# Retention attention and top-1 experts on one core: a token group's last tiles turned at the end of the next batch, and three PSUM tiles given other banks

## The chip, the core and the metric

The program runs on one core of one Trainium2 chip. The metric is the device time of that core in microseconds (us): 628.96 us, the median of three runs (627.0 to 629.3). The engines are named as the profile names them: PE (matrix products and transposes), DVE (vector engine), ACT (scalar engine), POOL (GpSimd), SP (the engine that issues most DMAs).

## The reference

```python
scores = scale * np.matmul(q, k.transpose(0, 1, 3, 2))      # 8 batches, 8 heads, 576 positions, head size 64
Dmat = np.where(rel >= 0, gamma[:, None, None] ** rel[None, :, :], 0.0)
ret = np.matmul(scores * Dmat[None], v)                     # no softmax: a decay by distance
x = ret.transpose(0, 2, 1, 3).reshape(B * S, H * D)         # 4608 tokens of 512
logits = xn @ en.T / tau                                    # 8 experts
expert_idx = np.argmax(logits, axis=1)
out[mask] = gate_w[mask, None] * (np.maximum(x[mask] @ w1[e], 0.0) @ w2[e])   # for each expert e
```

All is float32. The first part is linear attention with a decay; the second sends each token to one of eight experts, each of two weight matrices (512x1024 and 1024x512).

## The kernel before

**Two stages.** The first some 167 us are the attention, batch after batch; the rest are the eight experts, in which PE hardly pauses. The change lies in the attention.

**A batch.** Its 576 positions are four chunks of 128 and a tail of 64. Heads go in four pairs `p`. `emit_A(b, p)` (L584) makes the scores inside the chunks in two PSUM tiles `a` and DVE masks them (L599) into an SBUF tile `raw`. `emit_U(b)` (L607) makes k times v for each chunk, 32 products into two PSUM tiles `m`, which DVE sums up over the chunks into `Tst` (L627 once, L629 three times: the first of these frees the first of the two PSUM tiles, the third frees the second). `emit_QT` (L645) and `emit_O` (L663) add q times Tst and masked scores times v in a PSUM tile `o` per pair, and DVE scales it into `xT` and `xC` (`emit_X`, L677; lines L681, L683, L684). The tail has its own scores, `emit_At` (L686, masked by L695 into `pt`), and its own product, `emit_Ot` (L700): 16 products into two PSUM tiles, one for the even pairs and one for the odd, scaled by L722.

**The loop** (L809 to L860) runs over batches `b` and pairs `p`. At p = 0 the loads of batch b + 1 are issued and v of batch b + 1 is scaled on POOL (L567 four times, L571 once, `scale_v`). At p = 3 it already makes A and U of batch b + 1, since PE would else wait for their masks and sums. The load of v for batch b + 1 goes into the buffer that batch b - 1 used, so it waits for the tail product of b - 1.

**Token groups.** The tokens that batch b made are a group: 4 tiles of 128 tokens for an even batch, 5 for an odd one (`group_tiles`, L178). A group is worked off in the batch after its own, in tasks that `route_tasks` (L786) makes and the loop pops at the pairs in `SLOTS`: `route_logits` (L752), `route_tile` (L733: four transposes on PE into a PSUM tile `m`, a copy to SBUF on ACT, L744, a store to `xd` in DRAM by SP, L746, and a sum of squares on ACT, L748), `route_turn` (L766: the logits are transposed, DVE reduces them, L776), `route_head` (L182: six small DVE instructions, L194 to L202), `route_rank` and `route_onehot` (L243, L283) and `route_table` (L311). In each of batches 2 to 5 a quarter of the first expert's weights is split too: SP loads it, ACT rounds it (L168), DVE takes the rest (L169).

**Banks.** PSUM has eight banks: three tiles `a` (pool `psa`), two `o` (`pso`), three `m` (`psm`, shared by U, transposes, logits, tables and the tail). A tile takes a bank of its pool that another tile had before, and its first write waits until that tile has been read.

**Order.** Instructions are emitted in the loop's order, and a scheduler that goes by costs then interleaves them on each engine; each engine runs its row in that order, and waits where a semaphore has not come.

Of the kernel before, what the change touches and what calls it, by code (L numbers as in the profile page):

```python
# [9 lines left out]
F32 = mybir.dt.float32  # L10
# [8 lines left out]
P = 128  # L19
B, H, S, D = 8, 8, 576, 64  # L20
NP = H // 2
# [19 lines left out]
NW2 = 12  # L41
LAG = (3, 1)
POPS = (8, 3, 4, 0)
SLOTS = (0, 2)
NO = NT + 2


# [39 lines left out]
def retention_moe(ctx: ExitStack, tc: tile.TileContext, qk, kv, embT, tau, w1, w2, cst, out):  # L87
# [7 lines left out]
    psa = ctx.enter_context(tc.tile_pool(name="psa", bufs=3, space=PSUM))  # L95
# [20 lines left out]
    def behind():  # L116

        return ExitStack()
# [328 lines left out]
    with ExitStack() as att:  # L447
# [236 lines left out]
                nc.vector.tensor_tensor(out=x[:, p, : 512 - D], in0=po[:, D:], in1=gsb[:, p, D:512], op=ALU.mult)  # L684

        def emit_At(b):  # L686
            ps = psm.tile([P, 512], F32, name="m")
            u = ps[:, : NP * TL].rearrange("p (r n) -> p r n", r=NP)
            for p in range(NP):
                for h in range(2):  # L690
                    hs = slice(h * D, (h + 1) * D)
                    t = qkt[b, p]
                    mm(u[hs, p, :], t[hs, 1, 512:], t[hs, 0, 512:], start=True, stop=True)
            pt = a2.tile([P, NP, TL], F32, name="pt")
            nc.vector.tensor_tensor(  # L695
                out=pt, in0=u, in1=trit.unsqueeze(1).broadcast_to([P, NP, TL]), op=ALU.mult
            )
            Pt[b] = pt

        def emit_Ot(b):  # L700
            vt, T, pt = vtview(b), Tst[b % 2], Pt.pop(b)
            us = []
            for odd in range(2):
                ps = psm.tile([P, 512], F32, name="m")
                us.append(ps[:, : NP // 2 * TL].rearrange("p (r n) -> p r n", r=NP // 2))
            for r in range(NP // 2):
                for k in range(2):
                    for odd in range(2):
                        p = 2 * r + odd
                        for h in range(2):  # L710
                            hs = slice(h * D, (h + 1) * D)
                            mm(
                                us[odd][out_rows(p, h), r, :],
                                T[hs, NCH - 1, p, :] if k == 0 else vt[hs, p, :],
                                qkt[b, p][hs, 0, 512:] if k == 0 else pt[hs, p, :],
                                start=(r == 0 and k == 0),
                                stop=(r == NP // 2 - 1 and k == 1),
                            )
            x, xc = x_tiles(b)
            dst = xc[:, :, :TL] if b % 2 == 0 else x[:, :, 512 - D :]  # L720
            for odd in range(2):
                nc.vector.tensor_tensor(  # L722
                    out=dst[:, odd::2], in0=us[odd], in1=gsb[:, odd::2, 512:], op=ALU.mult
                )
# [27 lines left out]
        def route_logits(b):  # L752

            x = xT[b, "x"]
            lt = a1.tile([P, 5 * P], F32, name="lt")
            parts = [(x, 0, 512)] if b % 2 == 0 else [(x, P, 512), (xC[b // 2], 0, P)]
            for src, o, n in parts:
                ps = psm.tile([P, 512], F32, name="m")
                for p in range(NP):
                    mm(  # L760
                        ps[p * EW : (p + 1) * EW, :n], E32[:, p, :], src[:, p, :], start=True, stop=True
                    )
                nc.scalar.copy(lt[:, o : o + n], ps[:, :n])  # L763
            ltb[b] = lt
# [21 lines left out]
        def route_tasks(b):  # L786
            G = group_tiles(b)[1]
            tiles = [lambda g=g: route_tile(b, g) for g in range(G)]
            head = lambda: route_head(b)
            rank, table = (lambda: (route_rank(b), route_onehot(b))), (lambda: route_table(b))  # L790
            own = [lambda: route_logits(b)] + tiles[:2], tiles[2:] + [lambda: route_turn(b), head]

            first, second = owed or ([], [])
            owed[:] = [rank], [table]
            if b == B - 2:
                t = first + [lambda: (route_logits(b), route_turn(b))] + second + tiles[:2] + [head, rank]
                t += tiles[2:] + [table, lambda: slots_to_tokens(0, 3)]
                t += [lambda i=i: gather(0, i, group_tiles(B - 1)[0] * P) for i in range(3)]
                return t + [route_bump]
            return [own[0] + first, own[1] + second]  # L800

        tasks = []
        wq = wsplit_tasks(0)
# [5 lines left out]
        for b in range(B):  # L809
            for p in range(NP):  # L810
                if b + 1 < B:
                    load_qk(b + 1, p)
                    if p == 0:
                        load_v(b + 1)
                        load_k(b + 1)
                        scale_v(b + 1)
                if p + 1 < NP:
                    if b > 0 or p == 2:
                        with behind() if b > 0 else ExitStack():
                            emit_A(b, p + 1)  # L820
                else:
                    with behind():
                        if b + 1 < B:
                            emit_A(b + 1, 0)
                    with behind():
                        emit_At(b)
                    with behind():
                        if b + 1 < B:
                            emit_U(b + 1)
                if b == 0 and p == 0:  # L830
                    for r in range(NP):
                        turn_k(r)
                    emit_U(0)
                for _ in range(POPS[p] if b == B - 1 else 0):
                    if tasks:
                        tasks.pop(0)()
                if b == 0 and p < 2:
                    emit_O(b, p, True)
                    if p == 1:
                        emit_QT(b, 0, False)  # L840
                        emit_X(b, 0)
                        emit_X(b, 1)
                else:
                    if p % 2 == 0:
                        with behind():
                            emit_QT(b, p, True)
                    with behind() if b > 0 else ExitStack():
                        emit_O(b, p, False)
                    emit_X(b, p)
                if p == NP - 1:  # L850
                    with behind():
                        emit_Ot(b)
                if b < B - 1 and p in SLOTS and tasks:
                    with behind():
                        for task in tasks.pop(0):
                            task()
                if 1 < b < 6 and p == 1 and wq:
                    wq.pop(0)()
            if b < B - 1:
                tasks += route_tasks(b)  # L860
        b = B - 1
# [7 lines left out]
        first = [mm1_in(0, 0, 0)]  # L869
# [298 lines left out]
```

## Time and profile before

| | |
|---|---|
| median of the runs | 628.96 us (627.0 to 629.3) |
| the profiled execution | 627.92 us, span 626.1 us |
| PE busy | 609.4 us, 97% of the span |
| DVE, ACT, POOL busy | 54%, 35%, 29% |
| granted TensorE clock | 0.995 of 2.4 GHz in the mean |
| tail product ends, batches 1 to 6 | 47.96, 67.66, 87.69, 107.72, 127.96, 148.64 us |

In the timeline a row has the start, the time from the first start to the last end of the instructions merged in it, engine, line, operation, tiles (out<-in), their size and count; in brackets the engine's idle time just before and what ended it. A matmul in float32 leaves two records. Every product is recorded by the helper at L109 and every transpose by that at L113, so rows of PE are told apart by their tiles: `m<-ident,xT` is a token tile's transposes, `m<-ident,lt` those of the logits, `m<-rp,bt` the table, `a<-qkt` scores, `m<-qkt` (64x64) tail scores, `m<-vt,kt` U, `o<-raw,vt` the masked scores times v, `m<-qkt,Tst` and `m<-pt,vt` the tail product.

### The profile page before, as it was taken

The numbers are of one execution on the slowest core, as the hardware profiler recorded it, in microseconds if no ns is written. First come the engines' busy times: TensorE is split into PE (matmuls) and PEld (weight loads), VectorE is DVE, ScalarE is ACT, GpSimd is POOL, SyncE is SP. The second block draws the span as 40 slices with busy tenths as digits, with TensorE's granted clock in tenths as the row PEclk, the third lists the DMA queues.
The fourth block names the chain that finished last, engine by engine and source line by source line (L and its number), as shares of the span: only waits on it lengthen the run. The fifth ranks groups of instructions, "written<-read, shape, count | busy, mean of one in ns | idle before, by whom it ended". The sixth has DMA issues, their size and how long they took to land. (4 is left out here: it accounts for less than half of the span.)

```text
span 626.1 us, 12659 instructions
## 1 busy us (share of the span) xinstructions
PE 609.4 (97%) x5273; PEld 541.6 (87%) x5273; DVE 339.3 (54%) x687; ACT 216.7 (35%) x397; POOL 180.3 (29%) x165
## 2 busy tenths in 40 slices
PE   9999999989899999999999999999999999999995
PEld 8877778867698989889988998998899899889985
DVE  5676877768767776723670673368057426802200
ACT  1033333423444554423351433335143333512211
POOL 2522022220156636032313504241341324020011
PEclk9999999989999999999999999999999999999999
DMA  8899887972367895661483258147324824510001
GB/s 308 311 329 367 300 317 275 344 262 103 106 208 218 206 307 153 149 235 46 118 274 103 81 115 268 65 118 238 130 69 114 273 71 117 149 51 9 2 35 44
DMA packets 73275, 109.41 MB, mean 175 GB/s; under 512 B 44634, under 2 KB 45054, under 8 KB 71424
## 3 DMA queue, kind: packets, MB, share of 16 engines
q1 hardware_dynamic: 65536, 88.63, 44.1%
q0 software_dynamic: 7680, 19.95, 9.6%
q8 instruction: 42, 0.69, 0.4%
q14 instruction: 17, 0.14, 0.1%
HBM read 79.96 MB, written 19.94 MB: 160 GB/s over the span
## 5 line engine op out<-in xcount | busy, mean ns | idle before, releaser
L109 PE MATMUL a<-xs,wslot 128*128 128x384 f32 (+1 forms) x1536 | 227.8, 309 | 0.0
L109 PEld LDWEIGHTS a<-xs,wslot 128*128 128x128 f32 x1536 | 225.8, 189 | 0.7
L913 PE MATMUL o<-wslot,hs 128*128 128x512 f32 (+1 forms) x984 | 222.0, 386 | 0.0
L913 PEld LDWEIGHTS o<-wslot,hs 128*128 128x128 f32 x984 | 181.1, 188 | 38.3
L887 DVE SCALAR_TENSOR_TENSOR hs<-a,hs 128x384 fp32r<-128x384 f32 (+1 forms) x128 | 62.8, 490 | 170.6 <-ACT hs L886 167.8
L921 POOL DMA_INDIRECT out<-y,sid x40 | 43.4, 1086 | 225.1 <-ACT y L920 192.8
L886 ACT ACTIVATE hs<-a 128x384 fp32r<-128x384 f32 (+1 forms) x128 | 56.1, 439 | 127.3 <-PE a L109 117.3
L169 DVE TENSOR_TENSOR wslot<-raw,wslot 128x1024 fp32r<-128x1024 f32 x64 | 78.3, 1223 | 26.5 <-ACT wslot L168 25.4
L168 ACT CAST wslot<-raw 128x1024 fp32r<-128x1024 f32 x64 | 66.8, 1044 | 39.2 <-DMA raw<-w 39.2
L355 POOL DMA_INDIRECT raw<-xd,gid x40 | 41.6, 1041 | 88.8 <-DVE wslot L169 45.6
L920 ACT ACTIVATE y<-o,gt 128x512 f32<-128x512 f32 (+1 forms) x41 | 27.7, 677 | 110.5 <-PE o L913 94.7
L567 POOL TENSOR_TENSOR vt<-vt,cs 128x512 f32<-128x512 f32 x28 | 28.3, 1045 | 90.4 <-DMA vt<-kv 74.4
L366 POOL DMA_INDIRECT gt<-gd,gid x40 | 50.0, 1251 | 12.2 <-issue 12.2
L109 PE MATMUL a<-qkt 64*128 64x128 f32 x512 | 43.0, 291 | 2.5 <-DVE raw L599 2.5
L599 DVE TENSOR_TENSOR raw<-a,tri 128x512 f32<-128x512 f32 x64 | 41.4, 684 | 6.1 <-PE a L109 6.0
L109 PEld LDWEIGHTS a<-qkt 64*128 64x128 f32 x512 | 34.9, 189 | 7.5 <-DVE raw L599 3.9
L109 PE MATMUL o<-raw,vt 128*64 128x128 f32 x512 | 36.1, 280 | 0.0
L109 PEld LDWEIGHTS o<-raw,vt 128*64 128x64 f32 x512 | 28.2, 138 | 4.3 <-issue 3.2
L400 DVE COPY raw<-raw 128x1024 uint16<-128x1024 uint16 x37 | 28.2, 785 | 4.0 <-DMA raw<-raw 4.0
L744 ACT COPY y<-m 128x512 f32<-128x512 f32 x34 | 18.8, 586 | 32.5 <-PE m L113 32.4
L393 DVE COPY raw<-raw 128x1024 uint16<-128x1024 uint16 x37 | 26.0, 717 | 0.9 <-DMA raw<-xd,gid 0.9
L763 ACT COPY lt<-m 128x512 f32<-128x512 f32 (+1 forms) x12 | 5.4, 482 | 59.8 <-PE m L109 59.8
(127 smaller groups left out, 386.6 us busy)
## 6 DMA issues: line engine op xcount, KB each, us to landing
raw<-w SPq DMA_DIRECT2D x64, 512.0 KB, 4.8
qkt<-qk SPq DMA_DIRECT2D x32, 576.0 KB, 6.4
xd<-y SPq DMA_DIRECT2D x36, 256.0 KB, 3.5
vt<-kv SPq DMA_DIRECT2D x7, 1152.0 KB, 10.3
kt<-kv SPq DMA_DIRECT2D x7, 1024.0 KB, 5.0
vt<-kv SPq DMA_DIRECT2D x4, 256.0 KB
raw<-xd,gid POOLq DMA_INDIRECT x40
gt<-gd,gid POOLq DMA_INDIRECT x40
```

Source lines behind the costliest of these rows:

```text
L109: pe[:] = [nc.tensor.matmul(*args, **kw)]
L168: nc.scalar.copy(hi, raw)
L169: nc.vector.tensor_tensor(out=sl[:, 1, c * 1024 : (c + 1) * 1024], in0=raw, in1=hi.bitcast(F32), op=ALU.subtract)
L355: return nc.gpsimd.indirect_dma_start(out=t[:, :DM], out_offset=None, in_=xd[:rows, :], in_offset=bass.IndirectOffsetOnAxis(ap=gid[:, a : ...
L366: nc.gpsimd.indirect_dma_start(out=g[:, i : i + 1], out_offset=None, in_=gd[:, :], in_offset=bass.IndirectOffsetOnAxis(ap=gid[:, a : a + 1 ...
L400: nc.vector.tensor_copy(far.bitcast(U16).rearrange("p (n h) -> p h n", h=2), near.rearrange("p (h n) -> p h n", h=2))
L567: eng.tensor_tensor(out=v[:, c], in0=v[:, c], in1=g[:, c].unsqueeze(2).broadcast_to([P, H, D]), op=ALU.mult)
L599: nc.vector.tensor_tensor(out=pm[:, h], in0=ps[h].rearrange("p (c n) -> p c n", c=NCH), in1=tri.unsqueeze(1).broadcast_to([P, NCH, P]), op ...
L886: a = nc.scalar.activation(hi, ps[:, :n], AF.Relu)
L887: v = nc.vector.scalar_tensor_tensor(out=hs[:, 1, f, o : o + n], in0=ps[:, :n], scalar=0.0, in1=hi.bitcast(F32), op0=ALU.max, op1=ALU.subt ...
L913: nc.tensor.matmul(ps[:, :step], hs[:, hsp, f, i * P : (i + 1) * P], w[:, ws, f, n : n + step], start=(f == 0 and k == 0), stop=(f == NF - ...
L921: nc.gpsimd.indirect_dma_start(out=out[:, :], out_offset=bass.IndirectOffsetOnAxis(ap=sid[:, a : a + 1], axis=0), in_=y, in_offset=None, b ...
```

## The change

- The group's last token tiles (`tiles[2:]`: two of four, three of five) leave the second list of tasks, which is popped at p = 2, and become a third list of their own, popped at p = 3.
- At p = 3 the tasks are now emitted before the tail product and no longer behind it (before the change nothing was popped there).
- The tail scores (`emit_At`) take a tile `a`, the odd half of the tail product a tile `o`; both took a tile `m`.

```diff
-SLOTS = (0, 2)
+SLOTS = (0, 2, 3)
...
         def emit_At(b):
-            ps = psm.tile([P, 512], F32, name="m")
+            ps = psa.tile([P, 512], F32, name="a")
...
             for odd in range(2):
-                ps = psm.tile([P, 512], F32, name="m")
+                ps = pso.tile([P, 512], F32, name="o") if odd else psm.tile([P, 512], F32, name="m")
...
-            own = [lambda: route_logits(b)] + tiles[:2], tiles[2:] + [lambda: route_turn(b), head]
+            own = [lambda: route_logits(b)] + tiles[:2], [lambda: route_turn(b), head]
...
-            return [own[0] + first, own[1] + second]
+            return [own[0] + first, own[1] + second, tiles[2:]]
...
-                if p == NP - 1:
-                    with behind():
-                        emit_Ot(b)
                 if b < B - 1 and p in SLOTS and tasks:
                     with behind():
                         for task in tasks.pop(0):
                             task()
+                if p == NP - 1:
+                    with behind():
+                        emit_Ot(b)
```

PE at the end of batch 2, before the change (the group has five tiles, so 12 transposes are moved; an even batch's end has this shape):

```order
L113 MATMUL m<-ident,xT 128x128 x12
L113 MATMUL m<-ident,lt 128x128 x5
L109 MATMUL a<-qkt 128x128 x2
...
L109 MATMUL a<-qkt 128x128 x6
L109 MATMUL m<-qkt 64x64 x8
L109 MATMUL m<-vt,kt 64x64 x32
L109 MATMUL o<-raw,vt 64x128 x8
L109 MATMUL m<-qkt,Tst_196 64x64 x4
L109 MATMUL m<-pt,vt 64x64 x4
```

The same place after it:

```order
L113 MATMUL m<-ident,lt 128x128 x5
...
L109 MATMUL a<-qkt 128x128 x8
L109 MATMUL a<-qkt 64x64 x8
L109 MATMUL m<-vt,kt 64x64 x32
L109 MATMUL o<-raw,vt 64x128 x8
L113 MATMUL m<-ident,xT 128x128 x8
L109 MATMUL o<-qkt,Tst_196 64x64 x2
L109 MATMUL o<-pt,vt 64x64 x2
L113 MATMUL m<-ident,xT 128x128 x4
L109 MATMUL m<-qkt,Tst_196 64x64 x2
```

The transposes stood ahead of the logits' and now stand between U and the tail product, so all from the logits' transposes to U comes earlier by their time. The second of the moved tiles takes the bank of U's first half, and its first transpose waits for the first L629. The end of an odd batch has the same shape with two moved tiles.

DVE at the same end of batch 2, before:

```order
L776 TENSOR_REDUCE L_all<-m 128x32
L776 TENSOR_REDUCE L_all<-m 128x8
L194 TENSOR_REDUCE mx<-L_all 128x5
L169 TENSOR_TENSOR wslot_81<-raw,wslot_81 128x1024
...
L599 TENSOR_TENSOR raw<-a,tri 128x512
L201 TENSOR_TENSOR oh<-wm,wme 128x40
L202 TENSOR_SCALAR tok_all<-wm 128x5
L695 TENSOR_TENSOR pt<-m,trit 128x256
L627 COPY Tst_197<-m 128x256
L260 TENSOR_REDUCE s_1188<-oh 128x8
L629 TENSOR_TENSOR Tst_197<-m,Tst_197 128x256 x3
```

And after:

```order
L201 TENSOR_TENSOR oh<-wm,wme 128x40
L202 TENSOR_SCALAR tok_all<-wm 128x5
L260 TENSOR_REDUCE s_1188<-oh 128x8
L599 TENSOR_TENSOR raw<-a,tri 128x512
L169 TENSOR_TENSOR wslot_81<-raw,wslot_81 128x1024
L599 TENSOR_TENSOR raw<-a,tri 128x512
L695 TENSOR_TENSOR pt<-a,trit 128x256
L627 COPY Tst_197<-m 128x256
L629 TENSOR_TENSOR Tst_197<-m,Tst_197 128x256 x2
L681 TENSOR_TENSOR xT<-o,gsb 128x512
L629 TENSOR_TENSOR Tst_197<-m,Tst_197 128x256
```

L169, which needs a weight load and ACT's rounding of it, moved from ahead of the small instructions of `route_head` to between the two masks, so it still stands ahead of L695, L627 and L629; the scaling of pair 3's output (L681) slipped in ahead of the last L629.

SP at the end of batch 2, before (`xd<-y` are the token tiles' stores, `kt`, `qkt` and `vt` the loads for later batches):

```order
L746 DMA xd<-y 128x512 x3
L465 DMA kt<-kv 128x2048
L457 DMA qkt<-qk 128x1152 x2
L474 DMA vt<-kv 128x2304
L746 DMA xd<-y 128x512 x2
```

And after:

```order
L465 DMA kt<-kv 128x2048
L457 DMA qkt<-qk 128x1152
L746 DMA xd<-y 128x512 x3
L457 DMA qkt<-qk 128x1152
L474 DMA vt<-kv 128x2304
L746 DMA xd<-y 128x512 x2
```

The moved tiles' stores now stand behind the loads of k and of one pair, and directly ahead of the load of v.

## Rows read from the trace of the kernel before

**Rows 1.** The page's busy times, and PE's waits in the first 180 us by what ended them (total us, times, longest).

```profile
PE 609.4 (97%) x5273; PEld 541.6 (87%) x5273; DVE 339.3 (54%) x687; ACT 216.7 (35%) x397; POOL 180.3 (29%) x165
...
PE m L109 <- DVE pt L695: 2.6, 3, 1.0
...
PE m L109 <- DVE Tst L629: 1.7, 3, 0.6
```

**Rows 2.** Batch 3 by the windows view: its length, then busy time (and count) of PE, PEld, DVE, ACT and POOL, the granted clock, the share of the DMA engines and GB/s.

```profile
67.66:87.69 20.03, 18.33 (x330) 15.32 (x327) 16.20 (x43) 6.35 (x14) 4.62 (x5) 1.00 0.88 331
```

**Rows 3.** PE's timeline at the end of batch 3, from the moved tiles' transposes to the first scores behind the tail product.

```profile
79.15 1.09 PE L113 MATMUL m<-ident,xT 128*128 128x128 f32 x8
80.08 0.60 PE L113 MATMUL m<-ident,lt 128*128 128x128 f32 x4
...
80.79 1.16 PE L109 MATMUL a<-qkt 64*128 64x128 f32 x16
81.88 0.68 PE L109 MATMUL m<-qkt 64*64 64x64 f32 x16
82.49 2.08 PE L109 MATMUL m<-vt,kt 128*64 128x64 f32 x64
84.41 1.05 PE L109 MATMUL o<-raw,vt 128*64 128x128 f32 x16
86.20 0.33 PE L109 MATMUL m<-qkt,Tst 64*64 64x64 f32 x4 [0.75 <-DVE pt L695]
87.08 0.27 PE L109 MATMUL m<-qkt,Tst 64*64 64x64 f32 x2 [0.55 <-DVE Tst L629]
...
87.69 1.16 PE L109 MATMUL a<-qkt 64*128 64x128 f32 x16
```

**Rows 4.** DVE's timeline at the same end of batch 3.

```profile
80.72 0.29 DVE L776 TENSOR_REDUCE L_all<-m 128x32 f32<-128x128 f32 x1 [0.69 <-PE m L113]
...
81.28 0.34 DVE L195 TENSOR_TENSOR L_all<-L_all,mx 128x32 f32<-128x32 f32 x1
81.66 0.97 DVE L197 SCALAR_TENSOR_TENSOR w<-L_all,wme 128x32 f32<-128x32 f32 x1
...
83.39 1.23 DVE L169 TENSOR_TENSOR wslot<-raw,wslot 128x1024 fp32r<-128x1024 f32 x1
84.53 1.28 DVE L599 TENSOR_TENSOR raw<-a,tri 128x512 f32<-128x512 f32 x2
85.73 0.41 DVE L695 TENSOR_TENSOR pt<-m,trit 128x256 f32<-128x256 f32 x1
...
86.51 0.95 DVE L629 TENSOR_TENSOR Tst<-m,Tst 128x256 f32<-128x256 f32 x2
```

**Rows 5.** POOL's scaling of v (four pieces in a row) and ACT's rounding of the weights in batches 2 and 3, from their timelines.

```profile
56.64 4.05 POOL L567 TENSOR_TENSOR vt<-vt,cs 128x512 f32<-128x512 f32 x4 [12.09 <-DMA vt<-kv]
...
78.53 4.05 POOL L567 TENSOR_TENSOR vt<-vt,cs 128x512 f32<-128x512 f32 x4 [17.27 <-DMA vt<-kv]
...
61.62 1.05 ACT L168 CAST wslot<-raw 128x1024 fp32r<-128x1024 f32 x1 [0.56 <-DMA raw<-w]
...
82.31 1.05 ACT L168 CAST wslot<-raw 128x1024 fp32r<-128x1024 f32 x1 [0.77 <-DMA raw<-w]
```

**Rows 6.** PE's timeline at the end of batch 2.

```profile
59.30 1.53 PE L113 MATMUL m<-ident,xT 128*128 128x128 f32 x12
60.66 0.78 PE L113 MATMUL m<-ident,lt 128*128 128x128 f32 x5
...
67.66 1.16 PE L109 MATMUL a<-qkt 64*128 64x128 f32 x16
```

**Rows 7.** DVE's timeline at the end of batch 2.

```profile
61.33 0.39 DVE L776 TENSOR_REDUCE L_all<-m 128x32 f32<-128x128 f32 x2 [1.22 <-PE m L113]
...
62.70 1.23 DVE L169 TENSOR_TENSOR wslot<-raw,wslot 128x1024 fp32r<-128x1024 f32 x1 [0.76 <-ACT wslot L168]
...
66.49 1.40 DVE L629 TENSOR_TENSOR Tst<-m,Tst 128x256 f32<-128x256 f32 x3
```

**Rows 8.** SP's issues of the loads of v behind the tail products of batches 1 and 2, and of k.

```profile
48.15 0.37 SPq L474 DMA_DIRECT2D vt<-kv  x1
...
65.98 0.33 SPq L465 DMA_DIRECT2D kt<-kv  x1
...
68.04 0.61 SPq L474 DMA_DIRECT2D vt<-kv  x1
```

**Rows 9.** The end of batch 1: POOL's scaling of v, U on PE, and the first scores behind the tail product.

```profile
39.92 4.05 POOL L567 TENSOR_TENSOR vt<-vt,cs 128x512 f32<-128x512 f32 x4 [15.96 <-DMA xd<-y]
...
42.39 2.32 PE L109 MATMUL m<-vt,kt 128*64 128x64 f32 x64
...
47.96 1.16 PE L109 MATMUL a<-qkt 64*128 64x128 f32 x16
```

**Rows 10.** The granted clock behind the tail product of batch 5 (columns as in rows 2), and PE's timeline: the logits made in batch 4 (90.62) and in batch 6 (132.45), and the first scores behind the tail product of batch 5.

```profile
130.00:132.00 2.00, 2.00 (x34) 1.67 (x28) 0.95 (x2) 0.00 (x0) 0.00 (x0) 0.54 0.95 341
...
90.62 1.07 PE L109 MATMUL m<-xT,E 128*32 128x512 f32 x8
...
127.96 1.67 PE L109 MATMUL a<-qkt 64*128 64x128 f32 x16
132.45 1.06 PE L109 MATMUL m<-xT,E 128*32 128x512 f32 x8
```

## The prediction

> **What bounds the kernel now.** I read the busy times first: PE is busy 97% of the span, so there are 17 us of idle time to win in all [rows 1]. The list of PE's waits says where they can be won in the attention: the largest entries are three waits for L695 (2.6 us) and three for L629 (1.7 us) [rows 1]. PE's timeline puts both at one place, the tail product at the end of the odd batches 1, 3 and 5: at the end of batch 3 PE waits 0.75 us for the mask of the tail scores, whose bank the first half of the tail product takes, and 0.55 us for the first L629, whose bank the second half takes [rows 3]. Then DVE's timeline tells why these come late: DVE works without a pause from L776 at 80.72 to the last L629, in the order small routing instructions, weights (L169), two masks, L695, L627, L629 [rows 4]. DVE is the bound of a batch's end, PE of the rest: in batch 3 DVE is busy 16.2 of 20.0 us, PE 18.3 [rows 2]. Last I read POOL and ACT, for what DVE waits for there [rows 5].
>
> **The change part by part.** No instruction is added or taken away. PE's two waits go, as the masked tail scores and the odd half have banks of their own. The price is that the second moved tile now takes the bank of U's first half, so it waits for the same first L629, and that the stores, POOL and DVE meet in another order. I work out when the tail product ends, by the clock of the old trace, as if the batch began where it did.
>
> *Odd batches 3 and 5.* PE: the logits' transposes take the place of the moved tiles at 79.15, 0.93 us early. From their old start (80.08) to the end of O (84.41 + 1.05) is 5.38 us, so O ends at 84.5, the first moved tile (half of 0.93) at 85.0, and the second could begin. DVE: L776 and L195 also come 0.93 early, L195 at 80.35 [rows 4]. L195 and L197 do not last their 0.2 us in the old trace: L195 ends at 81.62 and L197 at 82.63, where POOL's pieces of v, 4.05 / 4 = 1.01 us each from 78.53, end (81.56 and 82.58) [rows 4, 5]. So they wait out POOL's piece; moved one piece ahead, they end at 80.6 and 81.6. Then a mask, L199 and a mask (0.6 + 0.2 + 0.6; two masks start-to-start take (85.73 - 84.53) / 2 = 0.6) to 83.0. L169 needs L168, which ends at 82.31 + 1.05 = 83.36 [rows 5]: 83.4 to 84.55 (1.14 to the next start). L201 and L202 0.25, L695 and L627 0.78 (85.73 to 86.51), L260 0.14, the first L629 0.42, and 0.15 until PE goes on (old: 86.51 + 0.42 to 87.08): 86.3. So the second tile waits 1.3 us, ends at 86.75, and the tail product, which without its waits takes about 0.7 (87.08 to 87.69 for 14 of its 16 products), ends at 87.45 instead of 87.69 [rows 3, 4]. That is -0.25; should L195 just miss a piece of POOL's, or v land later, it is up to +1.0. I take 0 for each.
>
> *Even batches 2 and 4.* Three tiles move, so PE's turn comes 60.66 - 59.30 = 1.36 us early [rows 6]. With 5.38 and 0.2 for a fifth transpose O ends at 64.9, the first moved tile at 65.35. On DVE, L776 comes at 59.97, L195 some 0.8 later at 60.75 [rows 7]. Now POOL: v's load is issued 48.15 - 47.96 = 0.2 us behind the tail product [rows 8, 9]. Now it stands behind two stores and one load on SP, and the second store waits for ACT's copy of a tile that ends just ahead of the tail product: at some 0.4 us an issue [rows 8], about 1.1 us later, and two stores of 256 KB more are in front of it. At the 331 GB/s of batch 3 [rows 2] these are 1.6 us, but the queue has a gap there. Bounds of v's delay: 0 (the gap takes all) to 2.7; I take 1.6. POOL then works from 58.24 to 62.9 (4.62 us [rows 2]) where it was done at 61.3, and the small instructions, 1.36 earlier, fall into it: L195 ends at 61.3, L197 at 62.35, L201 at 62.95, L260 at 63.2. A mask to 63.8. The weights' load is in the same queue, so L168 comes 1.6 late too, ends at 61.62 + 1.6 + 1.05 = 64.3, and L169, which stands ahead of the second mask, lasts to 65.5; second mask 66.1, L695 and L627 66.85, first L629 and release 67.4. The second tile waits 67.4 - 65.35 = 2.1 us and ends at 67.9; the odd half's first products (0.2) and the third tile follow, 68.5; the even half takes the bank of U's second half and needs the last L629, which L681 (0.6) now precedes: 67.3 + 0.5 + 0.6 + 0.4 + 0.15 = 69.0; the rest of the tail product 0.5: 69.5 against 67.66, +1.8. With v and weights on time (0) the same chain gives +0.3; with 2.7, +2.8. I take +1.7 each.
>
> *Batch 6* has no weights to split: without L169 and its wait the first L629 is through at 65.8, the last at 67; with the rest +0.6 (0 to +1.5).
>
> *Batch 1.* U waits for POOL already: POOL's fourth piece ends at 39.92 + 4.05 = 43.97, U's last quarter (0.5) can only follow it, and U's row lasts 2.32 us there against 2.08 in batch 3 [rows 3, 9]. U comes 0.93 earlier and still ends at 44.5, as v's load is where it was. O and one tile to 46.0; the small DVE instructions win one piece of POOL's (1.0), so the first L629 is through at 46.65, the second tile at 47.1, the last L629 at 47.5; then the whole tail product, 0.7: 48.25 against 47.96. +0.3 (-0.7 to +0.8).
>
> *Batches 0 and 7* move no tile. Their banks change where PE's row is in order anyway: 0 (within 0.5 either way).
>
> *The clock.* Behind the tail product of batch 5, PE ran at 0.54 of its clock, the lower level of 1.2 GHz for nearly all of that window; the stretch from the scores to the logits took 132.45 - 127.96 = 4.49 us against 90.62 - 87.69 = 2.93, so 1.56 us were lost [rows 3, 10]. Ahead of it PE had waited at the tail product as it does at the ends of batches 1 and 3 (2.6 + 1.7 us in three ends, 1.4 each [rows 1]); behind batch 3 the stretch shows no loss. I leave one such fall in, since the gaps do not shrink.
>
> Sum: 0.3 + 1.7 + 0 + 1.7 + 0 + 0.6 = +4.3. On the profiled execution, 627.92, that is 632.2; the median shown, 628.96, lies 1.04 above that execution, so 633.3.
>
> Two rules weigh on this. The trace shows the small DVE instructions held by POOL only at odd ends [rows 4, 5]. The Trainium skill (SBUF — State Buffer, section "Who interferes with whom") says that a DVE instruction with two SBUF inputs contends with a GpSimd instruction that reads SBUF and that the later one fully blocks. By it the moved ones are held at the even ends too, as the sum has it; without it batch 6 would lose 0.4 less and batches 2 and 4 nothing, as L169 is later anyway. And rows 8 with rows 5 show 8.5 us from issue (48.15) to POOL's start (56.64). The Trainium skill (DMA: Bandwidth & Descriptors, section "Queues, rings and completion order") says that each DMA engine takes descriptors in ring order: by that the stores put ahead of v delay it, and the +1.7 stands; if later transfers shared evenly, only the issue's 1.1 us would count, and it would be +1.2.
>
> **The rivals.**
> 1. *The tiles fill the wait, and the time falls.* The moved transposes need 0.93 us where PE idled 0.75 + 0.55 [rows 3]. If the first L629 is through by 85.0 in batch 3 instead of my 86.3, the second tile does not wait: the three odd ends win 4.3 us [rows 1], and with the gaps the clock's fall (1.56) goes: -5.9, 623.1. For it: DVE's head start. Against it: L169 can't start before 83.4, whatever comes earlier, and 2.7 us of DVE's chain stand behind it [rows 4, 5]. It decides at L168's end: the weights would have to land 1.3 us sooner.
> 2. *v and weights land on time.* DMA engines are busy 0.88 of batch 3 [rows 2], so there are gaps at the batch ends. Then the even ends cost 0.3, batch 6 0.2, batch 1 0.3, the odd ones win 0.25: +0.6, 629.6.
> 3. *The clock falls more often.* At the even ends PE would now idle 2.1 + 0.5 us, against 1.4 ahead of the one fall in the old trace. Two falls more: +4.3 + 3.1, 636.4.
>
> **How the numbers follow.** Forecast 0.53, rival 1 0.07, rival 2 0.22, rival 3 0.18. The time is the forecast's, 633.3. Its own range, with the bounds of the even ends and of v, is 630.5 to 635.5; for 8 in 10 it has to take in most of rivals 2 and 3: 628.8 to 637.2. What a measurement of this kernel can tell from no change is about 0.5%, 3.1 us. Faster by more: rival 1, 0.07. Slower by more: rival 3 and four fifths of the forecast, 0.18 + 0.42 = 0.60. The rest 0.33.
>
> **What would show it.** Right: PE waits of about 2 us at the second moved tile in batches 2 and 4 and about 1.3 in 3 and 5, put down to L629 or to L169's chain; no wait for L695; POOL's start in batch 2 later by 1 to 2 us than the old 8.7 behind the tail product; L195 and L197 stretched there. Wrong: no wait ahead of the moved tiles, tail products that end earlier in the odd batches, or v landing as before.

## The result and the profile after

The changed kernel takes 633.58 us, the median of 18 runs (631.59 to 638.31); the kernel before, run beside it as often, takes 630.33 us (627.0 to 633.95). The ratio is 1.0069, with a 95% interval of 1.0047 to 1.0090: 4.3 us slower, 3.0 to 5.7 (the means lie 4.3 us apart, the medians 3.2). The forecast was 633.3 us, which is 4.3 us over the median then known.

The profiled execution took 636.68 us (span 634.8), 3.1 us over its median. The spans differ by 8.7 us, and not all of that is the change. The windows view of the first 20 us, before and after (columns as in [rows 2]):

```profile
0.00:20.00 20.00, 18.58 (x221) 16.75 (x223) 11.78 (x36) 3.43 (x5) 7.33 (x10) 1.00 0.88 332
```

```profile
0.00:20.00 20.00, 16.34 (x155) 15.31 (x155) 10.24 (x32) 2.95 (x4) 4.49 (x8) 0.83 0.85 296
```

In this execution of the changed kernel PE idled 2.4 us until a load of q and k landed, and the granted clock of these 20 us was 0.83. The first product of q with Tst starts at 26.51 us instead of 21.18: 5.3 us are lost ahead of the first moved tile. The fastest run of the changed kernel took 631.59 us. So the batches are compared by their lengths, each from one batch's first scores behind a tail product to the next one's. First the windows view of before, for batches 2 and 4 to 6 (batch 3 is in [rows 2]), then that of after, for batches 2 to 6:

```profile
47.96:67.66 19.70, 19.10 (x340) 15.76 (x337) 14.34 (x40) 7.81 (x18) 4.62 (x5) 1.00 0.83 301
...
87.69:107.72 20.03, 19.11 (x341) 15.78 (x338) 14.39 (x40) 7.81 (x18) 4.62 (x5) 1.00 0.82 303
107.72:127.96 20.24, 18.33 (x330) 15.32 (x327) 16.34 (x43) 6.35 (x14) 4.62 (x5) 1.00 0.79 302
127.96:148.64 20.68, 20.32 (x341) 16.84 (x339) 14.40 (x40) 6.76 (x17) 4.62 (x5) 0.92 0.66 235
```

```profile
53.46:75.09 21.63, 19.21 (x344) 15.72 (x337) 16.62 (x38) 7.32 (x18) 4.62 (x5) 1.00 0.89 303
75.09:95.26 20.17, 18.43 (x333) 15.17 (x327) 15.97 (x42) 6.83 (x16) 4.62 (x5) 1.00 0.86 314
95.26:116.86 21.60, 19.25 (x344) 15.75 (x338) 16.62 (x39) 7.77 (x19) 4.62 (x5) 1.00 0.82 294
116.86:137.71 20.85, 18.82 (x334) 15.33 (x328) 15.99 (x42) 6.70 (x16) 4.62 (x5) 1.00 0.76 270
137.71:157.46 19.75, 18.93 (x345) 15.45 (x339) 14.82 (x38) 6.73 (x18) 4.62 (x5) 1.00 0.64 235
```

PE's busy time hardly differs in batch 2 (19.1 and 19.2), but DVE's grew by 2.3 us there, in 38 instructions instead of 40: some of them last longer. In batch 6 PE's busy time is smaller after, since the clock did not fall there this time (1.00 instead of 0.92).

PE's waits in the first 180 us after, as in [rows 1]:

```profile
PE m L113 <- DVE Tst L629: 4.8, 4, 2.1
...
PE m L113 <- DVE xC L683: 2.4, 2, 1.3
PE m L109 <- POOL vt L567: 1.5, 5, 0.3
```

The waits of the tail product are gone but for one of 0.4 us at the end of batch 1; a token tile's transposes (`m L113`) wait instead, 7.2 us in six places. PE's timeline after, at the ends of batches 2 and 3, answers to [rows 6, 3]:

```profile
70.23 0.66 PE L113 MATMUL m<-ident,xT 128*128 128x128 f32 x4
72.96 0.63 PE L113 MATMUL m<-ident,xT 128*128 128x128 f32 x4 [2.08 <-DVE Tst L629]
...
74.48 0.33 PE L109 MATMUL m<-qkt,Tst 64*64 64x64 f32 x4
...
92.07 0.66 PE L113 MATMUL m<-ident,xT 128*128 128x128 f32 x4
94.07 0.63 PE L113 MATMUL m<-ident,xT 128*128 128x128 f32 x4 [1.34 <-DVE xC L683]
```

At both ends the first moved tile runs at once and the second waits. In batch 3 the wait is put down to L683, a small DVE instruction that ends at 94.05; the L629 that frees the bank ends just before it, at 93.92. DVE's timeline after, at the end of batch 2, shows why L629 is late; it answers to [rows 7]:

```profile
66.18 0.51 DVE L195 TENSOR_TENSOR L_all<-L_all,mx 128x40 f32<-128x40 f32 x1
66.73 0.96 DVE L197 SCALAR_TENSOR_TENSOR w<-L_all,wme 128x40 f32<-128x40 f32 x1
67.72 0.20 DVE L199 TENSOR_REDUCE wm<-w 128x5 f32<-128x40 f32 x1
67.96 0.74 DVE L201 TENSOR_TENSOR oh<-wm,wme 128x40 bf16<-128x40 f32 x1
68.62 0.62 DVE L202 TENSOR_SCALAR tok_all<-wm 128x5 f32<-128x5 f32 x1
...
69.89 1.21 DVE L169 TENSOR_TENSOR wslot<-raw,wslot 128x1024 fp32r<-128x1024 f32 x1
71.02 0.68 DVE L599 TENSOR_TENSOR raw<-a,tri 128x512 f32<-128x512 f32 x1
...
72.39 0.95 DVE L629 TENSOR_TENSOR Tst<-m,Tst 128x256 f32<-128x256 f32 x2
```

L195, L197, L201 and L202, of some 0.2 us each, last 2.8 us together, each until POOL's next piece of v ends; the reduction L199 between them is not held. Then a mask, L169 and a mask follow. What stands behind that, from the timelines of POOL, ACT and SP after ([rows 5, 8]):

```profile
64.59 4.05 POOL L567 TENSOR_TENSOR vt<-vt,cs 128x512 f32<-128x512 f32 x4 [14.77 <-DMA vt<-kv]
...
68.41 1.05 ACT L168 CAST wslot<-raw 128x1024 fp32r<-128x1024 f32 x1 [7.59 <-DMA raw<-w]
...
53.62 0.86 SPq L746 DMA_DIRECT2D xd<-y  x2
54.57 2.02 SPq L457 DMA_DIRECT2D qkt<-qk  x1
56.70 0.38 SPq L474 DMA_DIRECT2D vt<-kv  x1
```

The load of v is issued 3.2 us behind the tail product of batch 1 (53.46) instead of 0.2, POOL starts 11.1 us behind it instead of 8.7, and ACT starts on the weights 14.95 us behind it instead of 13.66 (61.62 - 47.96).

At the other even end, batch 4, the same rows of SP and POOL, first before (its tail product ahead ended at 87.69), then after (95.26):

```profile
87.87 0.37 SPq L474 DMA_DIRECT2D vt<-kv  x1
...
96.73 4.05 POOL L567 TENSOR_TENSOR vt<-vt,cs 128x512 f32<-128x512 f32 x4 [13.59 <-DMA vt<-kv]
```

```profile
96.97 0.78 SPq L474 DMA_DIRECT2D vt<-kv  x1
...
106.35 4.05 POOL L567 TENSOR_TENSOR vt<-vt,cs 128x512 f32<-128x512 f32 x4 [15.26 <-DMA vt<-kv]
```

There the issue came 1.5 us later (1.71 behind the tail product instead of 0.18), and POOL 2.05 us later.

### The profile page after: what moved, and what is told of

Read it like the earlier page. It is cut to its first block, busy times and chain, and to the rows that moved or that the text cites. A ratio compares the mean times of both kernels' runs of the same rounds, so it can differ in the third digit from the quotient of the medians.

```text
span 634.8 us, 12655 instructions
## 1 busy us (share of the span) xinstructions
PE 610.9 (96%) x5273; PEld 541.8 (85%) x5273; DVE 345.5 (54%) x687; ACT 217.9 (34%) x397; POOL 180.8 (28%) x165
## 5 line engine op out<-in xcount | busy, mean ns | idle before, releaser
L169 DVE TENSOR_TENSOR wslot<-raw,wslot 128x1024 fp32r<-128x1024 f32 x64 | 78.2, 1222 | 27.9 <-ACT wslot L168 26.5
L168 ACT CAST wslot<-raw 128x1024 fp32r<-128x1024 f32 x64 | 66.8, 1044 | 68.6 <-DMA raw<-w 68.6
L109 PE MATMUL a<-qkt 64*128 64x128 f32 (+1 forms) x640 | 48.3, 282 | 4.8 <-DMA qkt<-qk 2.4
L109 PEld LDWEIGHTS a<-qkt 64*128 64x128 f32 (+1 forms) x640 | 40.5, 183 | 10.0 <-DVE raw L599 3.5
L599 DVE TENSOR_TENSOR raw<-a,tri 128x512 f32<-128x512 f32 x64 | 41.5, 681 | 11.7 <-PE a L109 11.7
L744 ACT COPY y<-m 128x512 f32<-128x512 f32 x34 | 19.5, 586 | 40.0 <-PE m L113 38.3
L113 PE MATMUL m<-ident,xT 128*128 128x128 f32 x128 | 19.3, 281 | 7.3 <-DVE Tst L629 4.8
```

Source lines behind the costliest of these rows:

```text
L109: pe[:] = [nc.tensor.matmul(*args, **kw)]
L168: nc.scalar.copy(hi, raw)
L169: nc.vector.tensor_tensor(out=sl[:, 1, c * 1024 : (c + 1) * 1024], in0=raw, in1=hi.bitcast(F32), op=ALU.subtract)
L599: nc.vector.tensor_tensor(out=pm[:, h], in0=ps[h].rearrange("p (c n) -> p c n", c=NCH), in1=tri.unsqueeze(1).broadcast_to([P, NCH, P]), op ...
```

## The experiments

All were timed beside the kernel before. In the table the third column is the ratio less one, times 630 us; the fourth adds up the lengths of batches 1 to 6 in the profiled execution, where the kernel before has 117.9 us without its clock's fall of 1.56 us. Executions of one kernel differ in the start, so the two columns needn't agree. Three of the lengths hold a fall of the granted clock to its lower level of 1.2 GHz. It cost some 3.0 us in e2 (batches 4 and 5), 1.55 in e5 (batch 4) and 1.5 in e11 (batches 2 and 3), reckoned as the prediction does it, by the stretch from the last tile or scores to the logits against the same stretch at the full clock.

| run | median us | against before, us | batches 1 to 6, us |
|---|---|---|---|
| the change | 633.58 | +4.3 (3.0 to 5.7) | 123.4 |
| e1_banks_alone | 630.47 | 0.0 (-1.7 to +1.8) | 118.2 |
| e2_tiles_alone | 638.56 | +9.0 (6.4 to 11.6) | 126.3 |
| e3_tiles_own_banks | 629.35 | -1.3 (-3.2 to +0.6) | 118.4 |
| e4_weights_behind | 633.09 | +3.7 (2.0 to 5.4) | 122.2 |
| e5_stores_behind_v | 635.00 | +6.6 (4.5 to 8.8) | 122.8 |
| e6_tiles_behind_tail | 638.04 | +8.0 (4.8 to 11.2) | 123.8 |
| e7_own_banks_weights | 625.15 | -4.0 (-5.7 to -2.3) | 116.5 |
| e8_with_stores_behind_v | 624.12 | -3.9 (-5.6 to -2.1) | 113.7 |
| e9_before_weights_behind | 625.44 | -5.2 (-7.2 to -3.3) | 116.6 |
| e10_own_banks_old_tail | 627.54 | -2.8 (-4.7 to -0.8) | 117.5 |
| e11_after_unscaled | 629.91 | -1.3 (-3.3 to +0.8) | 120.2 |
| e12_before_unscaled | 630.08 | -0.8 (-3.0 to +1.5) | 117.7 |

The third column holds the clock too. Over the 85 runs of the kernel before that stand beside these, 0.001 of mean granted clock goes with 0.66 us (a straight line through them, correlation -0.91). The medians of the mean granted clock are 0.9905 for e2 and e6 and 0.9915 for e5, 0.995 for the kernel before, and 0.996 to 0.9985 for e3, e4 and e7 to e10. As an estimate from that line, the distances at equal clock would be +5.0 (e2), +2.9 (e5), +4.5 (e6), -3.0 (e9) and -0.2 (e10). Whether an edit moved the clock or the executions differed in it is not separated.

**The banks alone** (the kernel before with the two changes of PSUM tiles, the tiles left at p = 2).

> Only the banks change: the tail scores in a bank of the scores' pool, the odd half of the tail product in a bank of the output's pool; the tiles keep their place. Theory A (the price of the change is the second moved tile's wait for the first half of U, with v and the weights late behind the stores): no tile is moved, so there is no price; PE's waits for L695 at the odd ends go, but L169 and L629 stand where they stood and the tail product still needs L629: 2 us under the kernel before to 1 us over it, and no wait longer than 1 us at a tile. Theory B (the banks themselves cost the time, since the tail now takes turns with scores and outputs): 3 to 4.5 us over the kernel before, as the changed kernel is. Theory C (the waits for L695 and L629 are what the banks were worth, and the tiles spoil it): 4 us under the kernel before or more.

No difference in time, as theory A had it; B and C fall. PE's waits show why nothing is won:

```profile
PE o L109 <- DVE xT L684: 2.1, 3, 0.9
...
PE o L109 <- DVE xT L681: 1.0, 2, 0.7
...
PE m L109 <- DVE pt L695: 0.7, 2, 0.4
```

The 4.3 us of waits for L695 and L629 at the odd ends [rows 1] have become 3.8 us. Of these 3.1 us are waits of the next batch's first outputs (`o`) for DVE's scaling, since the odd half now takes a bank from the output's pool; 0.7 us for L695 are left at the ends of batches 1 and 3, which A had gone.

**The order alone** (the changed kernel with all tail tiles in `m` again).

> Only the order changes: the last tiles of a group are turned at the batch's end ahead of the tail product; the tail keeps its old banks. Theory A: the second moved tile waits about 2 us in batches 2 and 4 and 1.3 in 3 and 5, as in the changed kernel, and the tail's halves meet the same banks once more behind it: 4 to 7 us over the kernel before, so no better than the changed kernel. Theory B (the banks cost it): within 1 us of the kernel before.

Worse than the changed kernel, as A had it and beyond its 7 us, but not by A's way: the first moved tile waits, 5.5 us for L695 in batches 2 to 4, where A had the second wait for L629. Behind one of these waits, of 1.69 us at the end of batch 4, the granted clock fell; PE's waits and the windows view:

```profile
PE m L113 <- DVE pt L695: 5.5, 3, 2.2
```

```profile
116.00:120.00 4.00, 4.00 (x58) 3.33 (x60) 1.08 (x3) 2.16 (x7) 0.00 (x0) 0.50 0.47 105
```

So the order costs the time. By the times the new banks take some of it back (9.0 against 4.3 us); by the lengths without the clock's fall e2 takes 123.3 us and the changed kernel 123.4, so that part may be the clock's.

**Own banks for the moved tiles.**

```diff
-            ps = psm.tile([P, 512], F32, name="m")
+            ps = psa.tile([P, 512], F32, name="a") if g >= 2 and b < B - 2 else psm.tile([P, 512], F32, name="m")
             for p in range(NP):
                 tr(ps[:, p * P : (p + 1) * P], src[:, p, :], ident)
```

> The changed kernel, but the moved tiles are turned in banks of the scores' pool instead of the one that U's halves use. Theory A1 (the bank that the second moved tile shares with U's first half is what costs): the waits of 2 and 1.3 us at the second tile go, 3.5 to 5 us less than the changed kernel, so within 1.5 us of the kernel before. Theory A2 (v and the weights land late, and DVE's chain to L629 sets the end whatever bank the tile has): the wait moves to the tail product and the time stays within 1 us of the changed kernel.

A1 holds: the price is gone. PE's timeline of this run at the end of batch 2:

```profile
66.17 0.66 PE L113 MATMUL a<-ident,xT 128*128 128x128 f32 x4
67.74 1.09 PE L113 MATMUL a<-ident,xT 128*128 128x128 f32 x8 [0.92 <-DVE raw L599]
```

The second tile now waits for a mask, 0.92 us instead of 2.08, and the third follows at once. POOL started as late as in the changed kernel (11.2 us behind the tail product), and the small instructions were held as there. So late v and late L169 cost the change its time by way of the tile's bank, which hung on L629; e9 below shows that L169 costs the kernel before too.

**The weights behind the tail product** (`if 1 < b < 6 and p == 1 and wq` becomes `p == 3`).

> The changed kernel, but the step of the weights in batches 2 to 5 (load, L168, L169) is issued behind the tail product instead of after the second pair of heads. Theory A with its term for L169 (it stands between the two masks of the next scores and waits for L168, so it delays the first L629): L629 comes about 1.2 us earlier at the ends of batches 2 to 5, but at the even ends the late v holds the small instructions as before: 0.5 to 2.5 us less than the changed kernel. Theory A1 (the bank alone): the tile waits only for L629, which comes 1.2 us earlier at four ends: 4 to 5 us less. Theory A2 without L169 (v alone): no change, within 0.5 us of the changed kernel.

The time is 0.7 us under the changed kernel's by the ratios, as theory A with its term for L169 had it (0.5 to 2.5), but their intervals of some 1.4 to 1.7 us don't tell that from nothing; by the profiles batches 2 and 4 are 0.8 and 1.0 us shorter and the six together 1.2. PE still waits 3.5 us for L629 at the tiles, in seven pieces of at most 1.0. A1's 4 to 5 us did not come.

**The stores behind v** (changed kernel; the stores of moved tiles are kept back until the loads of v and k of the next batch have been issued; the tiles `y` also get five buffers instead of three).

```diff
-            nc.sync.dma_start(out=xd[t * P : (t + 1) * P, :], in_=xw)
+            (held.append if g >= 2 and b < B - 3 else (lambda f: f()))(lambda: nc.sync.dma_start(out=xd[t * P : (t + 1) * P, :], in_=xw))
```

> The changed kernel, but the stores of the moved tiles stand on SP behind the next loads of v and k (in batches 1 to 5), with five buffers for turned tiles instead of three so that none of them has to wait for its store. Theory A with its term for v (the stores ahead of v delay its landing by some 1.6 us, POOL with it, and so the small DVE instructions at the even ends): v is issued within 0.4 us of the tail product again, POOL starts about 9 us behind it in batches 2 and 4 instead of 11, and the time is 1.5 to 3 us less than the changed kernel's. Theory A1 (the bank alone, v plays no part): within 0.7 us of the changed kernel, and the tile waits 2 us in batches 2 and 4 as before.

Theory A's gain of 1.5 to 3 us did not come by the times. The timelines of SP, POOL and ACT in this run, batch 2, whose first scores come at 50.77, then POOL's in batch 3 (first scores at 73.01) and the windows view of batch 4:

```profile
51.42 0.37 SPq L474 DMA_DIRECT2D vt<-kv  x1
51.88 5.31 SPq L746 DMA_DIRECT2D xd<-y  x4
...
57.94 0.59 SPq L165 DMA_DIRECT2D raw<-w  x1
...
61.60 4.05 POOL L567 TENSOR_TENSOR vt<-vt,cs 128x512 f32<-128x512 f32 x4 [13.45 <-DMA vt<-kv]
...
66.70 1.05 ACT L168 CAST wslot<-raw 128x1024 fp32r<-128x1024 f32 x1 [8.57 <-DMA raw<-w]
...
82.14 4.04 POOL L567 TENSOR_TENSOR vt<-vt,cs 128x512 f32<-128x512 f32 x4 [15.92 <-DMA vt<-kv]
```

```profile
93.57:115.42 21.85, 20.79 (x344) 17.03 (x339) 15.09 (x39) 7.75 (x19) 4.62 (x5) 0.92 0.83 285
```

v is issued 0.65 us behind the tail product, and POOL starts 10.8 us behind it, not 9 (10.2 in batch 4); after it was 11.1 in both. In batches 3 and 5 v gained more: POOL starts 9.1 and 8.8 us behind instead of 11.4 and 12.4. The 10.2 us from v's issue to POOL's start in batch 2 say nothing of the stores: in the kernel before that trip takes 8.5 to 10.5 us over batches 1 to 6. The weights, now behind four stores, reach ACT 15.93 us behind the tail product instead of 14.95 (later by 0.4 and 0.65 in batches 3 and 4, sooner by 0.9 in batch 5): the second tile waits 2.68 us in batch 2. So v landed sooner and some of the delay went to the weights. What that is worth stays open. By the times e5 lies 2.3 us over the changed kernel, with intervals that overlap. By the lengths it lies 2.2 us under it (121.3), once the fall of the clock in batch 4 is taken out, which came behind a tile's wait of 1.87 us.

**The tiles behind the tail product** (the two `if` blocks swapped back, the third list kept).

> The changed kernel with the moved tiles turned behind the tail product instead of ahead of it. Theory A1 (a tile ahead of the tail product needs a bank that is not free yet; behind it the banks are free): the tiles do not wait, and the time is within 1.5 us of the kernel before. Theory A with v's term and the chain to L629: the tail product now waits for L629 itself, with nothing in that wait, and the stores still stand ahead of v's load, later than before: 2 to 5 us over the kernel before.

A1 falls, A comes near (its 5 us lie inside the interval). The tiles wait for L629 in this place too, 3.5 us in eight pieces, and the tail product itself waits 3.2 us, for L695 and not for A's L629:

```profile
PE m L113 <- DVE Tst L629: 3.5, 8, 0.8
PE m L109 <- DVE pt L695: 3.2, 4, 1.1
```

**Own banks, old tail banks, weights behind**, and the same **with the stores behind v**.

> The moved tiles ahead of the tail product in banks of the scores' pool, the tail scores and both halves of the tail product in the old banks, and the step of the weights behind the tail product. Theory A (a tile's bank, then L169's chain, then v): with the bank and L169 out of the way the order itself is worth something: 2 to 5 us under the kernel before. A rival (whatever is moved, DVE's sum of work in a batch sets its end): within 1 us of the kernel before.

> As the run with the tiles in banks of the scores' pool, old tail banks and the weights behind, and the moved tiles' stores behind the loads of v and k, with five buffers for turned tiles. Theory A with v's term: another 1 to 1.5 us less, so 3 to 6.5 us under the kernel before. Without v's term: the same as that run.

Both beat both kernels. In e7 the 12 transposes at the end of batch 2 run without a wait, in e8 too; e8's batches 1 to 6 are 2.8 us shorter than e7's, but its further gain is not told from zero by the times (624.12 and 625.15 us with the kernel before beside both), so they don't decide on v's term.

**The kernel before with the weights behind**, and **own banks with the weights in place**.

> The kernel before with one edit: the step of the weights in batches 2 to 5 is issued behind the tail product. No tile is moved and no bank changes. Theory A (L168 and L169 were already what DVE's chain to L629 waited for at the ends of the kernel before): 2 to 3.5 us under the kernel before, with PE's waits for L695 and L629 at the odd ends down to under 0.5 us each. Rival (the weights only matter where a moved tile waits for L629): within 1 us of the kernel before.

> The moved tiles ahead of the tail product in banks of the scores' pool, the tail in the old banks, the weights in their place. Theory A (order and banks are worth little while L168 sets DVE's chain): 0 to 2 us under the kernel before. Rival (the order with free banks is what made the run with own banks and weights behind faster): 3 to 5 us under the kernel before, as that run.

The first is the plainest gain of all: 5.2 us with one number changed and no tile moved (the upper part of it goes beyond theory A; its interval reaches A's 3.5). In the profile the batches 2 to 5, where the edit acts, are 2.6 us shorter, which lies within A's 2 to 3.5. PE's waits at the tail product went at the end of batch 3 and stayed at those of batches 1 and 5, 2.1 us in all instead of 4.3:

```profile
PE m L109 <- DVE Tst L629: 1.1, 2, 0.6
PE m L109 <- DVE pt L695: 1.0, 2, 0.6
```

The second came out between the two theories, 2.8 us under the kernel before. With the weights behind, the order with own banks adds nothing to e9 that the times show (e7: -4.0).

**Both kernels without POOL's scaling of v.**

```diff
-                        scale_v(b + 1)
+                        pass
```

> The changed kernel without POOL's scaling of v from batch 1 on (that part of the computation is left out), so nothing of POOL's runs while the small DVE instructions do. Theory A as forecast (at the even ends L169 is later than what POOL holds, so POOL's part is about 0.4 us in batch 6 alone): the distance to the kernel before without the same scaling stays at 3 to 4 us. Rival (the small instructions held by POOL are the price of the order): the distance falls to 0.5 to 2 us.

> The kernel before without POOL's scaling of v from batch 1 on (left out here as in the run of the changed kernel), for the difference between the two. Theory A: 0 to 1.5 us under the kernel before, since the odd ends lose only the hold of L195 and L197, which L168 covers. Rival (POOL's hold is on the path): 2 us or more under it.

The distance between the two is -0.5 us by the ratios (interval about 3.0 either way) and +2.5 by the lengths of batches 1 to 6, where with the scaling it is +4.3 and +5.5. Theory A's 3 to 4 is not what came by the first reading, and the second holds a fall of the granted clock in e11 alone, from the end of batch 2 (behind a tile's wait of 2.22 us) into batch 3; the windows view of batch 3:

```profile
69.37:90.46 21.09, 19.80 (x330) 16.57 (x328) 14.94 (x42) 6.50 (x15) 0.00 (x0) 0.94 0.77 272
```

Its scores-to-logits stretch took 4.13 us against 2.94 after, and the end of batch 2 lost 0.3 us more. Without these 1.5 us the distance by the lengths is +1.0, inside the rival's 0.5 to 2. It is no clean difference even so: in e12's batch 2 U waited 1.64 us for ACT's copy L744 behind a late L168, which is not so in the kernel before. By itself e12 is 0.8 us under the kernel before, as A had it, but its interval takes in the rival's 2 too. DVE's timeline of the changed kernel without scaling, end of batch 2:

```profile
59.99 0.20 DVE L195 TENSOR_TENSOR L_all<-L_all,mx 128x40 f32<-128x40 f32 x1
60.23 0.20 DVE L197 SCALAR_TENSOR_TENSOR w<-L_all,wme 128x40 f32<-128x40 f32 x1
...
60.69 0.20 DVE L201 TENSOR_TENSOR oh<-wm,wme 128x40 bf16<-128x40 f32 x1
60.81 0.17 DVE L202 TENSOR_SCALAR tok_all<-wm 128x5 f32<-128x5 f32 x1
...
63.82 1.23 DVE L169 TENSOR_TENSOR wslot<-raw,wslot 128x1024 fp32r<-128x1024 f32 x1 [2.07 <-ACT wslot L168]
```

Without POOL the four instructions last 0.8 us instead of 2.8, and DVE then waits 2.07 us for L168; the second tile still waits 2.22 us. In batches 1, 5 and 6 the changed kernel is 0.1 to 0.4 us ahead; in batches 2 to 4 it is 0.8 to 1.4 us behind, of which the clock's fall made 0.3 in batch 2 and 1.2 in batch 3.

## Why the prediction was right, and where it was not

The step that carried it held: the second moved tile waits for the first L629, whose chain the forecast followed through the small instructions, L169, the masks, L695 and L627.

| end of batch | change forecast | change in the profiles | second tile's wait, forecast | measured |
|---|---|---|---|---|
| 1 | +0.3 | +0.64 | | 0.39 |
| 2 | +1.7 | +1.93 | 2.1 | 2.08 |
| 3 | 0 | +0.14 | 1.3 | 1.34 |
| 4 | +1.7 | +1.57 | 2.1 | 2.00 |
| 5 | 0 | +0.61 | 1.3 | 1.01 |
| 6 | +0.6 | +0.63 | | 0.36 |
| sum | +4.3 | +5.5 | | |

(Batch 6 without the 1.56 us of the clock in the old trace: 19.75 - 19.12.)

- *No wait for L695 at the odd ends:* right; the row is gone. That the second tile's wait for DVE's chain would fill what this gives back, so that the odd ends win nothing, is right too. In e1, with no tile moved, the banks win nothing either, there because PE waits for the scaling. (The prediction calls the waits for L695 and L629 the largest entries; it passes over 2.5 us for L599 in seven pieces of at most 0.4, which stay at 2.4 after.)
- *Rival 1* (the tiles fill the wait) fell where the prediction put its point of decision: L168 started 14.65 us behind the tail product in batch 3 before, 15.23 after, later and not sooner.
- *Rival 2* (v and weights on time) fell: v, POOL and L168 were all late at the even ends.
- *The stores ahead of v.* The effect was within its bounds and its cause in part another. POOL started 2.45 and 2.05 us later at the even ends (forecast: 1.6 for v's landing, 0 to 2.7). The issue came later by 3.0 us in batch 2 and 1.5 in batch 4, not 1.1; in batch 2 SP stood 2.02 us in one issue of a load. The trip from issue to POOL's start was 0.6 us shorter in batch 2 (7.9 against 8.5) and 0.5 longer in batch 4 (9.4 against 8.9), although stores lay ahead. The Trainium skill (DMA: Bandwidth & Descriptors, section "Queues, rings and completion order") says that descriptors are taken in ring order, from which the prediction had the stores lengthen the trip; these two trips don't show such a lengthening, within the 8.5 to 10.5 us that the trip takes in the kernel before. What set it was not separated.
- *"Batches 2 and 4 nothing, as L169 is later anyway":* this step was wrong by a little in after's trace. L168 ended at 69.46, DVE was through with what stood ahead of L169 at 69.89, so POOL's hold was the later one by 0.4 us (in batch 4 too: 111.21 and 111.65). The rule itself (the Trainium skill, SBUF — State Buffer, section "Who interferes with whom") agrees with the rows: L195, L197 and L201, with two SBUF inputs, are held to the ends of POOL's pieces, and last 0.20 us without POOL. The runs without scaling bear out the step for batches 2 and 4 and put POOL's part elsewhere. At the even ends the price stays without POOL, since L169 waits for L168 instead: 1.4 us of 1.6 in batch 4, and in batch 2 some 0.65, which would be 2.3 but for e12's own wait of 1.64. In batches 1, 5 and 6 it goes: 1.9 us together become -0.7. So POOL's part is some 2.5 us by the lengths, against the 0.4 us in batch 6 alone that the sum gave it, and by the times the distance fell by 4.8 us (about 3.3 either way). In after's batches 1 and 5 POOL also makes U wait (0.25 to 0.32 us in five places).
- *Batch 5* is a term that was too small, though inside its bound of +1.0: its weights came late as well, L168 starting 15.90 us behind the tail product instead of 14.86, and v too, POOL starting 12.4 instead of 10.5. Its v was issued 2.6 us later behind the tail product than before. The forecast had the late transfers at even ends only.
- *Batch 1* can't be judged: e9 has the same instructions as the kernel before up to its end, and took 20.05 us there against 18.80. So a single batch's 0.6 us, in batches 5 and 6 too, is not told from the scatter of executions; the 1.9 and 1.6 us of batches 2 and 4 stand with the waits that make them.
- *The clock.* One fall of 1.56 us was left in, and in the profiled execution there was none behind a tail product, in spite of waits of 2.08 and 2.00 us; but e2, e5 and e11 each had one shortly behind a tile's wait, of 1.69, 1.87 and 2.22 us, and e5 none behind one of 2.68. So what rival 3 names does happen in kernels close to this one. This one execution does not bear it out, and whether the falls became more or fewer over all runs stays open: the median over runs of the mean granted clock was 0.994 for the changed kernel (18 runs) and 0.995 for the kernel before (85 runs beside the experiments), and in the two profiles the first 20 us alone make such a difference.

So the mechanism held: the moved tile's bank, the chain to L629 and the even ends as the dear ones. That the total was met to a tenth of a microsecond is luck: the measured 4.3 has an interval of 3.0 to 5.7, the batches add up to +5.5, the fall of the clock that was left in did not come in the profile, batch 5 was put at nothing, and v's delay was more of the issue and less of the trip than the sum had it.

## What to carry to other kernels

Before work is moved into a gap, look at which bank, buffer or queue place it takes and who gives that free: here the moved transposes fitted into PE's idle time, but took the bank whose release was itself what PE idled for, and with banks of their own (e3) the loss was gone. When a tail waits for the end of a chain on another engine, shorten that chain first: taking one 1.2 us instruction and its late load out of DVE's chain (e9, 625.44 us) was worth more than the moved tiles with banks of their own (e10, 627.54 us, timed beside it).

## What was not expected of the hardware

- Stores and loads reordered on one queue exchanged delays in part: with v's load ahead of four stores (e5), POOL started on v 0.3 and 0.9 us sooner than in the changed kernel in batches 2 and 4 and 2.3 and 3.6 sooner in 3 and 5, and the weights reached ACT up to 1.0 us later in batches 2 to 4. In one and the same kernel (before) the trip of such a load took 8.5 to 10.5 us.
- A DVE instruction with a single SBUF input, L202, was held by POOL too: 0.62 us at the end of batch 2 after, ending with POOL's last piece, against 0.17 without POOL (e11). The reduction L199, 0.20 us, never was.
- The first scores behind batch 0's tail product came at 29.05 us in the earliest profile (e8) and at 34.02 in the latest (after), with a granted clock of 1.00 and 0.83 in the first 20 us: more than the whole change is worth, so only lengths inside the program could be compared row by row.
